# Agent attention with a cosine feed-forward on one core: two bursts of exponentials a batch instead of three

## The chip, the core and the metric

The kernel runs on one core of a Trainium2 chip. The metric is the device time of one execution in microseconds (us), the median of several runs. The engines are named as in the profile: PE (TensorE, matrix products), PEld (its weight loads), DVE (VectorE), ACT (ScalarE), POOL (GpSimd) and SP (SyncE, which issues transfers).

## What is computed

Cut from the reference, with B = 4 batches of N = 12480 tokens, C = 128 features, 49 agents and a hidden width of 2048:

```python
def sm(a, b):
    s = scale * (a @ b.transpose(0, 2, 1))
    s = s - s.max(-1, keepdims=True)
    e = np.exp(s)
    return e / (e.sum(-1, keepdims=True) + 1e-09)
agent_v = sm(agents, k) @ v
x = sm(q, agents) @ agent_v
...
h = x @ w_in
out = (h * np.cos(h)) @ w_out
```

So there are two softmaxes, one of the agents over all keys of a batch and one of each query over the 49 agents, and behind them a wide layer whose activation is h cos h.

## The kernel before

Queries and keys are taken in groups of 960 tokens (8 tiles of 120), 13 groups a batch and 52 in all. The product of a batch's agent values with w_in is made once a batch (`project`), into one of two tables `a`, so that the hidden layer of a group of queries is one product of that table with the group's transposed softmax weights `pT`.

**The main loop** goes over 832 steps. A group takes 16 steps, a batch 208. A step is a slice of 256 hidden units for 480 tokens: PE makes the first product into a buffer `ph` of PSUM (L853, two instructions, three buffers), ACT the cosine (L856, `c`), DVE the cubic part (L862, `r` = (cos - 1) h), and PE, four steps later, the second product (L878), which gathers 8 steps in one buffer `one`. There are two buffers `one`, and scores, values and transposes use the same two. The cubic part frees the step's `ph`.

**Around the steps lies the softmax work of what comes next**: the scores of keys and queries (`scores`, L152, one transfer and 8 products for a group), copied out of PSUM by ACT, or inside a burst by DVE (L527), the queries' maximum on DVE (L531) and its subtraction on POOL (L533), the running maximum of the keys (L250), and for the keys, once all 13 groups are scored, `top`, `across`, `spread`, `shift`: the maximum is spread over partitions (`mxb`, L271) and subtracted on POOL (L275). After the exponential the keys' groups go through `add` (POOL, L284 and L286, into `es`) and `values` (PE, L301, the products with v; DVE adds them up, L307 and L309). Queries go through their sums (L578) and reciprocals (L582, L583) on DVE, the weights on POOL (L591, `p`), a transpose on PE (L600), a copy on ACT (L604) and two casts and two differences on POOL (L607, L608) into `pT`.

**Bursts.** Exponential and sine lie in different tables of ACT, so a change between them costs a table load each way. The exponentials are therefore made in bursts: one exponential for a *piece* (some groups of queries, side by side in one tile `e`) and one for a *lot* (some groups of keys), between two table loads. The tuple `BURSTS` has the steps of a batch at which they stand; `pieces` says which groups of queries, `lots` which groups of keys. A burst is planned for step n; ACT reaches it after the cosine of step n + 1.

**The order** is written by hand. `plan(n, f)` runs f at step n, `early_plan` likewise ahead of the step's cubic part, `extra` puts it at the next free step of certain places among 8, and `spread_out` spreads a list over the steps up to an end. In a *window* of six steps from a burst on, PE, DVE and ACT keep the order in which the code was written (`as_traced`); `fill` puts there what DVE and PE are to do while ACT has the exponential's table: the piece's sums, and up to three items of the list `todo`, each a group of query scores ("q") or a group of values ("v").

Of the kernel before, what the change touches and what calls it, by code (L numbers as in the profile page):

```python
# [18 lines left out]
P = 128  # L19
TT = 120  # L20
# [22 lines left out]
def agent_attention_cos_ffn(ctx, tc, qT, kT, v, v0, v0_rest, agT, w_in, w_out, outT):  # L43
# [122 lines left out]
    class Weights:  # L166
# [43 lines left out]
        def turned(self, c):  # L210

            pt = self.psum()
            for t in range(4):
                f = slice((4 * c + t) * P, (4 * c + t + 1) * P)
                nc.tensor.transpose(pt[:, t * P:(t + 1) * P], win[:, f], ident)
            if c == 0:
                self.room = self.sb.tile([P, NF, P], F32, name="e", bufs=4)
            wt = self.done[c, 0] = self.room[:, 4 * c:4 * c + 4]
            nc.scalar.copy(wt.rearrange("p f d -> p (f d)"), pt)

# [255 lines left out]
    with ExitStack() as pools:  # L476
# [28 lines left out]
        NQ = NB * NG  # L505
        NSTEP = NB * PER
        e_of, rz_of = {}, {}
        PIECES = 5

        def query_parts(n, piece, wide=False, by_vector=False):  # L510
            b, g = n // NG, n % NG
            src = qT[b, :, g * GRP:(g + 1) * GRP]
            if wide:
                ps = scores_twice(sb.tile([P, 2 * 512], F32, name="xt", bufs=3)[:, :GRP], src, b, pair())
                yield
            else:
                ps = scores(sb, src, b, small()).rearrange("p (h t) a -> p h t a", h=2)
                yield
            if n == piece[0]:
                e = sb.tile([TT, PIECES * GT, NA], F32, name="e", bufs=4)  # L520
                rz = sb.tile([TT, PIECES * GT], F32, name="rz2", bufs=4)
                for i, k in enumerate(piece):
                    e_of[k], rz_of[k] = e[:, i * GT:(i + 1) * GT], rz[:, i * GT:(i + 1) * GT]
                    e_of[piece], rz_of[piece] = e[:, :len(piece) * GT], rz[:, :len(piece) * GT]
            e = e_of[n].rearrange("p (h t) a -> p h t a", h=2)
            if not wide:
                (nc.vector.tensor_copy if by_vector else nc.scalar.copy)(e, ps)  # L527
                ps = e
            mx = sb.tile([TT, GT], F32, name="mx2")
            mx = mx.rearrange("p (h t) -> p h t", h=2)  # L530
            nc.vector.reduce_max(mx, ps, axis=AX.X)  # L531
            on = nc.vector if wide else nc.gpsimd
            on.tensor_sub(e, ps, mx.unsqueeze(3).to_broadcast([TT, 2, HT, NA]))  # L533

        def query_first(n, piece):

            e = e_of[n] = sb.tile([TT, GT, NA], F32, name="e", bufs=4)
            rz = rz_of[n] = sb.tile([TT, GT], F32, name="rz2", bufs=4)
            ps = scores_twice(wide_tile()[:, :GRP], qT[0, :, n * GRP:(n + 1) * GRP], 0, pair())
            yield  # L540
# [78 lines left out]


        assert NG == 13
        BURSTS = (109, 133, 157)
        WINDOW = 6
        windows = set()

        def windows_late(n):
            return any(n - x in windows for x in (1, 2, 3, 4))

        first, early = (0, 1, 2), (3, 4, 5, 6, 7)
        pieces = [tuple(tuple(range(b * NG + x, min(b * NG + y, NQ))) for x, y in ((8, 12), (12, 16), (16, 21))  # L630
                        if b * NG + x < NQ) for b in range(NB)]
        lots = [(0, 4), (4, 4), (8, 5)]


        po_w = []
# [133 lines left out]
        for b in range(1, NB):  # L769
# [12 lines left out]
            t = extra(t, ab[b].across)  # L782
            t = extra(t + 1, ab[b].spread)
            assert t < o + BURSTS[0], (t, o)
            for g, n in lots:
                plan(t, ab[b].shift, g, n, nc.gpsimd)
            nxt = scored(pieces[b][0], False, True)[:2]
            ahead = len(nxt)
            fresh = [scored(ps[1], False, True), scored(ps[2], False, True), nxt]
            for k, at in enumerate(BURSTS):  # L790
                at += o
                burst(at, ps[k], (ab[b], *lots[k]))
                vs, qs = valued(k - 1) if k else [], fresh[k]
                todo = []
                for x in ("qqqqqqq", "vq", "vq")[k]:
                    z = vs if x == "v" else qs
                    if z:
                        todo.append(z.pop(0))
                fill(at, todo)
                t = at + 6  # L800
                if k == 2:
                    vs += valued(2)
                qs, todo = todo, []
                qs += [x for x in fresh[k] if x not in qs]
                qs = [x[:3] if x[0] is query else x for x in qs]
                while vs or qs:
                    todo += qs[:1] + vs[:1]
                    vs, qs = vs[1:], qs[1:]
                if k == 0:
                    todo += [x[:3] for x in fresh[1][:2]]  # L810
                    del fresh[1][:2]
                end = o + BURSTS[min(k + 1, 2)] - 4
                for i, x in enumerate(todo):
                    t = extra(t, *x, dense=k == 2) + (2 if k == 2 else 1)
                    assert k == 2 or x[0] is not query or t < o + BURSTS[k + 1], (t, o, k)
                    if k < 2 and i + 1 < len(todo):
                        t += max(0, (end - t) // (len(todo) - i - 1) - 1)
            plan(t, ab[b].total)
            t = extra(t, ab[b].folded) + 1
            t = extra(t, ab[b].inverse) + 1  # L820
# [240 lines left out]
```

## Time and profile before

| what | value |
|---|---|
| median of 3 runs | 1180.17 us (1177.71 to 1183.73) |
| profiled execution | 1180.92 us |
| its span, first to last instruction | 1179.1 us |
| busy: PE, DVE, ACT, POOL | 95%, 90%, 83%, 30% |
| cubic parts (L862) | 832, 916.1 us busy |
| cosines (L856) | 832, 785.3 us busy |
| loads of the exponential's table in bursts (L575) | 11 |

The span is made of the start, four batches of 208 steps and an end. A batch's extra work lies in the three first batches; the last has only its own remaining queries to prepare. Busy shares are averages over stretches with different limits. In rows of a timeline the first two numbers are the start and the duration in us, equal neighbours are merged (x2), and the bracket at the end is the engine's idle time before the row and what ended it.

### The profile page before, as it was taken

Reading aid. Unit: us, or ns where it says so; the run is one execution under the profiler, and the core shown is the slowest. Engines: PE = TensorE matmul, PEld = TensorE weight load, DVE = VectorE, ACT = ScalarE, POOL = GpSimd, SP = SyncE. Lnnn points to the kernel's source line nnn. Section 1 sums busy time; section 2 is a strip of 40 time slices with the busy share of each in tenths; the row PEclk is TensorE's granted clock in tenths of the full one; section 3 lists DMA queues with packets and bytes.
Section 4 is the critical chain, followed back from the end, with each engine's and each line's share of the span. In section 5 each row is a group of like instructions: output and inputs, shape, how many; then the busy total and the mean of one; then the engine's idle time right before and its main releaser. Section 6 shows DMA issues by size and latency. Waiting matters only on the chain.

```text
span 1179.1 us, 17151 instructions
## 1 busy us (share of the span) xinstructions
PE 1122.9 (95%) x6239; PEld 901.8 (76%) x6239; DVE 1061.0 (90%) x1205; ACT 980.1 (83%) x1234; POOL 349.9 (30%) x389
## 2 busy tenths in 40 slices
PE   6899999999999999999899999998999999989996
PEld 3677888787778888787777888877777777767774
DVE  5779999997899999998789999998878999999996
ACT  4778888898678888888778888898777899998995
POOL 1032131752313131463323122264331223122320
PEclk9999999998999999999899999999989999999998
DMA  9733324523201223263220322354240000000001
GB/s 362 288 93 108 101 84 135 167 85 106 96 34 54 91 74 95 81 181 114 85 84 17 101 67 84 106 152 130 68 118 34 34 34 18 34 17 34 18 34 37
DMA packets 37520, 107.74 MB, mean 91 GB/s; under 512 B 4162, under 2 KB 4770, under 8 KB 37426
## 3 DMA queue, kind: packets, MB, share of 16 engines
q1 hardware_dynamic: 37426, 106.55, 28.0%
q8 instruction: 52, 0.85, 0.3%
q14 instruction: 42, 0.34, 0.1%
HBM read 80.97 MB, written 25.56 MB: 90 GB/s over the span
## 4 chain that ended last, share of the span: by engine, by line
PE 70%; DVE 15%; ACT 9%; issue 4%; DMA 1%; SPq 0%; POOL 0%; ACTq 0%; DVEq 0%
PE ph L853 26%; PE one L878 22%; DVE r L862 12%; PE one L152 10%; ACT c L856 5%; PE one L301 3%; PE one L874 2%; PE one L600 2%; PE one L875 1%; DMA c<-qT 1%; PE ph L451 1%; PE one L346 1%; ACT osb L880 1%; ACT L575 1%; ACT s L279 1%
## 5 line engine op out<-in xcount | busy, mean ns | idle before, releaser
L862 DVE SCALAR_TENSOR_TENSOR r<-c,ph 128x960 fp32r<-128x960 f32 x832 | 916.1, 1148 | 60.3 <-ACT c L856 49.7
L856 ACT ACTIVATE c<-ph 128x960 f32<-128x960 f32 x832 | 785.3, 980 | 110.9 <-PE ph L853 99.3
L853 PE MATMUL ph<-pT,a 113*128 113x480 f32 x1664 | 540.2, 404 | 19.7 <-DVE r L862 18.4
L878 PE MATMUL one<-r,w 128*128 128x480 f32 x1664 | 505.4, 392 | 2.1 <-ACT osb L880 1.7
L853 PEld LDWEIGHTS ph<-pT,a 113*128 113x128 f32 x1664 | 293.8, 191 | 134.9 <-DVE r L862 73.6
L878 PEld LDWEIGHTS one<-r,w 128*128 128x128 f32 x1664 | 312.3, 192 | 54.9 <-issue 4.8
L152 PEld LDWEIGHTS one<-ag,xt 128*120 128x120 f32 x1408 | 164.3, 188 | 14.1 <-DVE sums L307 4.2
L152 PE MATMUL one<-ag,xt 128*120 128x49 f32 x1408 | 160.9, 268 | 5.5 <-DVE sums L307 3.0
L591 POOL TENSOR_TENSOR p<-e,rz 120x392 f32<-120x392 f32 x51 | 42.9, 846 | 323.7 <-PE one L600 252.2
L608 POOL TENSOR_TENSOR pT<-p,pT 49x480 fp32r<-49x480 f32 x102 | 124.2, 1217 | 7.8
L533 POOL TENSOR_TENSOR e<-e,mx 120x392 f32<-120x392 f32 x49 | 41.4, 844 | 225.9 <-DVE mx L531 225.6
L607 POOL CAST pT<-p 49x480 fp32r<-49x480 f32 x102 | 59.4, 583 | 114.7 <-ACT p L604 110.1
L880 ACT COPY osb<-one 128x480 f32<-128x480 f32 x104 | 57.9, 557 | 4.1 <-PE one L878 4.1
L301 PE MATMUL one<-vt,s 120*49 120x128 f32 (+1 forms) x624 | 44.9, 289 | 5.2 <-DVE sums L309 5.2
L301 PEld LDWEIGHTS one<-vt,s 120*49 120x49 f32 (+1 forms) x624 | 35.1, 136 | 17.9 <-issue 8.1
L286 POOL TENSOR_TENSOR es<-es,s 120x392 f32<-120x392 f32 x36 | 36.8, 1023 | 37.2 <-ACT s L279 35.5
L275 POOL TENSOR_TENSOR s<-s,mxb 120x1568 f32<-120x1568 f32 (+1 forms) x9 | 31.5, 3534 | 34.1 <-DVE mxb L271 34.1
L875 PE MATMUL one<-pT,b 113*128 113x480 f32 x104 | 39.9, 384 | 0.0
L874 PE MATMUL one<-pT,b 113*128 113x480 f32 x104 | 39.9, 384 | 0.0
L248 ACT COPY s<-one 120x392 f32<-120x392 f32 x36 | 17.5, 487 | 20.8 <-PE one L152 20.8
L527 ACT COPY e<-one 120x392 f32<-120x392 f32 x34 | 16.6, 487 | 20.3 <-PE one L152 20.3
L600 PEld LDWEIGHTS one<-ident,p 120*113 120x113 f32 x204 | 28.6, 179 | 4.6 <-ACT a L347 0.9
(143 smaller groups left out, 542.7 us busy)
## 6 DMA issues: line engine op xcount, KB each, us to landing
outT<-osb SPq DMA_DIRECT2D x51, 480.0 KB, 2.6
xt<-qT SPq DMA_DIRECT2D x49, 480.0 KB, 3.6
xt<-kT SPq DMA_DIRECT2D x39, 480.0 KB, 3.5
vt<-v SPq DMA_DIRECT2D x78, 240.0 KB, 3.9
xt<-kT SPq DMA_DIRECT2D x7, 512.0 KB, 7.7
vt<-v SPq DMA_DIRECT2D x6, 512.0 KB, 5.2
c<-kT SPq DMA_DIRECT2D x5, 512.0 KB, 6.9
vt<-w_in SPq DMA_DIRECT2D x8, 256.0 KB, 7.2
```

The costliest lines, as they stand in the source:

```text
L152: mm = nc.tensor.matmul(ps[:, t, :], xt[:, t * TT:(t + 1) * TT], ag[:, b, :], start=True, stop=True)
L301: mm = nc.tensor.matmul(po[h * HI:h * HI + width], e[:, x * NA:x * NA + width], vt[:, x, :], start=(t == 0), stop=(t == HT - 1))
L600: mm = nc.tensor.transpose(pt[:KR, t * TT:(t + 1) * TT], p_in[n % 2][:, t, :KR], ident[:TT, :TT])
L607: nc.gpsimd.tensor_copy(pT[own, c], p[own])
L608: nc.gpsimd.tensor_sub(pT[other, c], p[own], pT[own, c].bitcast(F32))
L853: nc.tensor.matmul(ph[:, j, :CH], ai[:, f], pTs[q % 3][:, c], start=True, stop=True)
L856: nc.scalar.activation(cos, h, AF.Sin, bias=HALF_PI, scale=1.0)
L862: nc.vector.scalar_tensor_tensor(r, cos, 1.0, h, op0=ALU.subtract, op1=ALU.mult)
L874: nc.tensor.matmul(po, b1[k], pTs[q % 3][:, c], start=False, stop=False)
L875: nc.tensor.matmul(po, b2[k], pTs[q % 3][:, c], start=False, stop=False)
L878: nc.tensor.matmul(po, w1[:, f, :], r[:, j, :], start=(f == 0), stop=(f == NF - 1))
L880: nc.scalar.copy(osb[:, c * CH:(c + 1) * CH], po)
```

## The change

Each batch has two bursts, at steps 97 and 142, instead of three at 109, 133 and 157. The pieces become 6 and 7 groups of queries (of 4, 4 and 5), the lots 7 and 6 groups of keys (of 4, 4 and 5). The tile `e` holds seven groups instead of five and has three buffers instead of four; the three first groups share one. The shift of the keys is cut into four parts (4, 3, 3, 3) instead of three. Three groups of the next batch's queries are scored ahead instead of two, and two groups of the first lot's values wait for the second window, whose list is "qvq". The exponentials cover the same elements.

```diff
-        PIECES = 5
+        PIECES = 7
...
-                e = sb.tile([TT, PIECES * GT, NA], F32, name="e", bufs=4)
+                e = sb.tile([TT, PIECES * GT, NA], F32, name="e", bufs=3)
...
-            e = e_of[n] = sb.tile([TT, GT, NA], F32, name="e", bufs=4)
+            if n == 0:
+                e_of["first"] = sb.tile([TT, 3 * GT, NA], F32, name="e", bufs=3)
+            e = e_of[n] = e_of["first"][:, n * GT:(n + 1) * GT]
...
-        BURSTS = (109, 133, 157)
+        BURSTS = (97, 142)
...
-        pieces = [tuple(tuple(range(b * NG + x, min(b * NG + y, NQ))) for x, y in ((8, 12), (12, 16), (16, 21))
+        pieces = [tuple(tuple(range(b * NG + x, min(b * NG + y, NQ))) for x, y in ((8, 14), (14, 21))
...
-        lots = [(0, 4), (4, 4), (8, 5)]
+        lots = [(0, 7), (7, NG - 7)]
...
-            for g, n in lots:
+            for g, n in ((0, 4), (4, 3), (7, 3), (10, 3)):
                 plan(t, ab[b].shift, g, n, nc.gpsimd)
-            nxt = scored(pieces[b][0], False, True)[:2]
+            nxt = scored(pieces[b][0], False, True)[:3]
             ahead = len(nxt)
-            fresh = [scored(ps[1], False, True), scored(ps[2], False, True), nxt]
+            fresh, kept = scored(ps[1], False, True), []
             for k, at in enumerate(BURSTS):
                 at += o
                 burst(at, ps[k], (ab[b], *lots[k]))
-                vs, qs = valued(k - 1) if k else [], fresh[k]
+                vs, qs = kept, fresh
                 todo = []
-                for x in ("qqqqqqq", "vq", "vq")[k]:
+                for x in ("qqq", "qvq")[k]:
...
-                if k == 2:
-                    vs += valued(2)
...
+                vs += valued(k)
+                if k == 0:
+                    vs, kept = vs[:-2], vs[-2:]
+                end = o + (BURSTS + (182,))[k + 1] - 4
...
-                    t = extra(t, *x, dense=k == 2) + (2 if k == 2 else 1)
+                    t = extra(t, *x, dense=k == 1) + 1
```

On ACT, at the first burst of the second batch, the order before is this; `e` is a piece and `s` a lot, and the numbers are partitions x elements.

```order
L856 ACTIVATE c<-ph 128x2x480 x2
L880 COPY osb<-one 128x480
L856 ACTIVATE c<-ph 128x2x480 x2
L575 ACT_TABLE_LOAD
L575 ACTIVATE e<-e 120x1568
L279 ACTIVATE s<-s 120x1568
L856 ACT_TABLE_LOAD
L856 ACTIVATE c<-ph 128x2x480 x5
```

At the first burst of the second batch of the change ACT has this order:

```order
L880 COPY osb<-one 128x480
L856 ACTIVATE c<-ph 128x2x480 x7
L577 ACT_TABLE_LOAD
L577 ACTIVATE e<-e 120x2352
L279 ACTIVATE s<-s 120x2744
L856 ACT_TABLE_LOAD
L856 ACTIVATE c<-ph 128x2x480 x2
```

Both exponentials are longer, and between the copy of a group's output and the burst seven cosines stand instead of two.

On DVE, at the third burst of the second batch, the order before is this; `rz` is the sums of a piece, `one` is scores for L527 and values for L309.

```order
L862 SCALAR_TENSOR_TENSOR r<-c,ph 128x960 x6
L309 TENSOR_TENSOR sums<-sums,one 113x128 x2
L578 TENSOR_REDUCE rz_5225<-e 120x8 x2
L527 COPY e<-one 120x392
L531 TENSOR_REDUCE mx_5726<-e 120x8
L578 TENSOR_REDUCE rz_5225<-e 120x8 x3
L862 SCALAR_TENSOR_TENSOR r<-c,ph 128x960 x5
```

At the second and last burst of the second batch of the change DVE has this order:

```order
L309 TENSOR_TENSOR sums<-sums,one 113x128
L862 SCALAR_TENSOR_TENSOR r<-c,ph 128x960
L527 COPY e<-one 120x392
L531 TENSOR_REDUCE mx_5546<-e 120x8
L580 TENSOR_REDUCE rz_4885<-e 120x8 x2
L309 TENSOR_TENSOR sums<-sums,one 113x128
L580 TENSOR_REDUCE rz_4885<-e 120x8 x5
L862 SCALAR_TENSOR_TENSOR r<-c,ph 128x960 x2
```

The copy of the scores stands ahead of the sums instead of among them, one addition of values has moved ahead of the last cubic part, and the sums are seven instead of five.

On POOL, from the shift of the second batch on, the order before is this; `e` in L533 is a group of queries, `es` the sum of the keys' exponentials, `p` the weights of a group and `pT` what PE reads.

```order
L275 TENSOR_TENSOR s<-s,mxb 120x1568 x2
L275 TENSOR_TENSOR s<-s,mxb 120x1960
L607 CAST pT_97<-p 49x480 x2
L608 TENSOR_TENSOR pT_97<-p,pT_97 49x480 x2
L533 TENSOR_TENSOR e<-e,mx_4993 120x392
L284 COPY es<-s 120x392
L286 TENSOR_TENSOR es<-es,s 120x392
L533 TENSOR_TENSOR e<-e,mx_5017 120x392
L286 TENSOR_TENSOR es<-es,s 120x392 x2
L533 TENSOR_TENSOR e<-e,mx_5052 120x392
```

From the shift of the second batch of the change on, POOL has this order:

```order
L275 TENSOR_TENSOR s<-s,mxb 120x1568
L275 TENSOR_TENSOR s<-s,mxb 120x1176 x3
L533 TENSOR_TENSOR e<-e,mx_4887 120x392
L533 TENSOR_TENSOR e<-e,mx_4911 120x392
L284 COPY es<-s 120x392
L286 TENSOR_TENSOR es<-es,s 120x392 x6
L533 TENSOR_TENSOR e<-e,mx_4952 120x392
L593 TENSOR_TENSOR p_102<-e,rz_2754 120x2x4x49
L593 TENSOR_TENSOR p_101<-e,rz_2754 120x2x4x49
L533 TENSOR_TENSOR e<-e,mx_5001 120x392
L609 CAST pT_97<-p 49x480 x2
L610 TENSOR_TENSOR pT_97<-p,pT_97 49x480 x2
```

The next `pT` stood right behind the shift and now stands behind all of the lot's additions, two products and four subtractions. In both versions it is the one that PE needs at step 112.

## Rows read from the trace of the kernel before

**Rows 1.** The page, part 1: busy us (share of the span) and instructions.

```profile
PE 1122.9 (95%) x6239; PEld 901.8 (76%) x6239; DVE 1061.0 (90%) x1205; ACT 980.1 (83%) x1234; POOL 349.9 (30%) x389
```

**Rows 2.** Stretches: length, busy PE PEld DVE ACT POOL, clock, DMA; second batch, two third bursts.

```profile
365.50:648.00 282.50, 275.07 (x1579) 227.91 (x1579) 259.04 (x288) 239.01 (x286) 93.83 (x99) 0.98 0.30 91
...
288.00:301.00 13.00, 11.43 (x50) 9.63 (x50) 7.08 (x13) 8.89 (x8) 5.89 (x6) 0.61 0.39 115
...
569.00:587.00 18.00, 14.65 (x83) 12.03 (x83) 12.53 (x19) 13.59 (x14) 7.10 (x7) 0.81 0.28 82
```

**Rows 3.** Timeline of DVE, first burst of the second batch.

```profile
497.88 2.22 DVE L862 SCALAR_TENSOR_TENSOR r<-c,ph 128x960 fp32r<-128x960 f32 x2 [0.17 <-ACT c L856]
...
500.68 0.56 DVE L531 TENSOR_REDUCE mx<-e 120x8 f32<-120x392 f32 x1
501.56 1.03 DVE L578 TENSOR_REDUCE rz<-e 120x8 f32<-120x392 f32 x2 [0.32 <-ACT e L575]
...
505.25 2.22 DVE L862 SCALAR_TENSOR_TENSOR r<-c,ph 128x960 fp32r<-128x960 f32 x2 [0.53 <-ACT c L856]
```

**Rows 4.** Timeline of DVE, second burst of the second batch.

```profile
533.21 2.22 DVE L862 SCALAR_TENSOR_TENSOR r<-c,ph 128x960 fp32r<-128x960 f32 x2 [0.17 <-ACT c L856]
...
540.58 1.15 DVE L862 SCALAR_TENSOR_TENSOR r<-c,ph 128x960 fp32r<-128x960 f32 x1 [0.58 <-ACT c L856]
```

**Rows 5.** Timeline of DVE, third burst of the second batch.

```profile
567.10 4.41 DVE L862 SCALAR_TENSOR_TENSOR r<-c,ph 128x960 fp32r<-128x960 f32 x4 [0.59 <-ACT c L856]
...
579.69 5.48 DVE L862 SCALAR_TENSOR_TENSOR r<-c,ph 128x960 fp32r<-128x960 f32 x5
585.09 0.18 DVE L582 TENSOR_SCALAR rz<-rz 120x40 f32<-120x40 f32 x1
586.42 1.15 DVE L862 SCALAR_TENSOR_TENSOR r<-c,ph 128x960 fp32r<-128x960 f32 x1 [1.15 <-ACT c L856]
```

**Rows 6.** Timeline of DVE, third burst of the first batch.

```profile
287.82 1.15 DVE L862 SCALAR_TENSOR_TENSOR r<-c,ph 128x960 fp32r<-128x960 f32 x1
288.89 0.28 DVE L309 TENSOR_TENSOR sums<-sums,one 113x128 f32<-113x128 f32 x1
...
296.21 0.57 DVE L527 COPY e<-one 120x392 f32<-120x392 f32 x1 [3.74 <-PE one L152]
...
298.76 2.21 DVE L862 SCALAR_TENSOR_TENSOR r<-c,ph 128x960 fp32r<-128x960 f32 x2
```

**Rows 7.** Timeline of DVE, third burst of the third batch.

```profile
862.85 0.57 DVE L527 COPY e<-one 120x392 f32<-120x392 f32 x1 [3.74 <-PE one L152]
```

**Rows 8.** Timeline of ACT, first burst of the second batch.

```profile
498.73 1.28 ACT L575 ACT_TABLE_LOAD   x1
...
504.25 2.79 ACT L856 ACTIVATE c<-ph 128x960 f32<-128x960 f32 x3
```

**Rows 9.** Groups by line and shape: busy us, mean ns | idle before.

```profile
L575 ACT ACT_TABLE_LOAD x11 | 14.1, 1283 | 0.2
...
L575 ACT ACTIVATE e<-e 120x1568 f32<-120x1568 f32 x7 | 10.6, 1511 | 0.1
...
L575 ACT ACTIVATE e<-e 120x1960 f32<-120x1960 f32 x4 | 7.3, 1836 | 0.0
...
L583 DVE RECIPROCAL rz<-rz 120x32 f32<-120x32 f32 x7 | 2.4, 341 | 0.0
```

**Rows 10.** Timeline of PE, third burst of the second batch.

```profile
575.31 1.79 PE L152 MATMUL one<-ag,xt 128*120 128x49 f32 x16
```

**Rows 11.** Timeline of POOL, shift and first burst of the second batch.

```profile
491.44 10.51 POOL L275 TENSOR_TENSOR s<-s,mxb 120x1568 f32<-120x1568 f32 x3 [13.48 <-DVE mxb L271]
...
503.19 2.49 POOL L608 TENSOR_TENSOR pT<-p,pT 49x480 fp32r<-49x480 f32 x2
...
507.14 1.03 POOL L286 TENSOR_TENSOR es<-es,s 120x392 f32<-120x392 f32 x1
...
513.37 1.65 POOL L591 TENSOR_TENSOR p<-e,rz 120x392 f32<-120x392 f32 x2 [1.50 <-DVE rz L583]
```

More of the change, by code (lines that the diff above doesn't have):

```diff
@@ L216, in turned @@
             if c == 0:
-                self.room = self.sb.tile([P, NF, P], F32, name="e", bufs=4)
+                self.room = self.sb.tile([P, NF, P], F32, name="e", bufs=3)
             wt = self.done[c, 0] = self.room[:, 4 * c:4 * c + 4]
@@ L800, in agent_attention_cos_ffn @@
                 t = at + 6
-                if k == 2:
-                    vs += valued(2)
-                qs, todo = todo, []
-                qs += [x for x in fresh[k] if x not in qs]
-                qs = [x[:3] if x[0] is query else x for x in qs]
+                qs = [x[:3] for x in qs]
+                vs += valued(k)
+                if k == 0:
+                    vs, kept = vs[:-2], vs[-2:]
+                end = o + (BURSTS + (182,))[k + 1] - 4
+                todo = []
                 while vs or qs:
@@ L808, in agent_attention_cos_ffn @@
                     vs, qs = vs[1:], qs[1:]
[L809 to L812, printed above, removed]
                 for i, x in enumerate(todo):
-                    t = extra(t, *x, dense=k == 2) + (2 if k == 2 else 1)
-                    assert k == 2 or x[0] is not query or t < o + BURSTS[k + 1], (t, o, k)
-                    if k < 2 and i + 1 < len(todo):
+                    t = extra(t, *x, dense=k == 1) + 1
+                    if i + 1 < len(todo):
                         t += max(0, (end - t) // (len(todo) - i - 1) - 1)
+                assert k or t <= at - o + o + BURSTS[1] - BURSTS[0], (t, o)
+                fresh = nxt
             plan(t, ab[b].total)
```

## Prediction

> **What bounds the kernel now.** I read the busy shares first. PE is busy 95% and DVE 90% of the span [rows 1], so neither has much to give, and ACT, on which the exponentials run, isn't the fullest. The table by stretch says the same of one batch: in the second, of 282.5 us, PE has work in 275.07 and DVE in 259.04 [rows 2]. DVE runs one cubic part (L862) a step and everything else between them; a batch can't be shorter than DVE's work plus the time in which DVE is kept from it. So the question is where DVE goes without cubic parts, and the timeline of DVE around each burst of exponentials answers it.
>
> While ACT loads the exponential's table, runs two exponentials and loads the sine's table again, no cosine is made. DVE finishes the cubic parts whose cosines are there and then has only what the program put into the burst: sums of the exponentials, and copies and maxima of the scores that PE makes meanwhile. I call the time from the end of the last cubic part before to the start of the next one a gap. In the second batch the first burst's gap runs from 497.88 + 2.22 = 500.10 to 505.25, 5.15 us [rows 3], the second's from 535.43 to 540.58, 5.15 us [rows 4]. The third is longer: 571.51 to 579.69, 8.18 us, and six steps later DVE waits once more, 1.15 us, for a late cosine [rows 5]. In the first batch the third gap is 288.97 to 298.76, 9.79 us [rows 6], with a wait of 3.74 us of DVE's copy for PE's scores; the third batch has the same 3.74 [rows 7], and I take 9.79 there too. The first two bursts I take at 5.15 in all three batches.
>
> The third gap isn't long for ACT's sake. PE makes two groups of values there before the scores that DVE's copy waits for, and the granted clock is low: 0.61 of full speed in that stretch of the first batch, in which PE is busy for 11.43 of 13.00 us, and 0.81 in the second's [rows 2]. A part of it therefore ran at the lower of the two levels, 1.2 GHz instead of 2.4.
>
> **The change, part by part.** *What goes.* Three batches lose one burst of three each. Six gaps of 5.15, two of 9.79 and one of 8.18 + 1.15 make 59.8 us in which cubic parts stood still.
>
> *What comes in their place.* Six bursts, each longer. Between the two starts that bracket it, 498.73 (table load) and 504.25 (first cosine after), the old first burst keeps ACT for 5.52 us [rows 8]. It held 1568 + 1568 elements; the new ones hold 2352 + 2744 or 2744 + 2352, so 1960 more. 392 more elements cost 1836 - 1511 = 325 ns [rows 9], or 0.83 ns each, so 1.63 us, and the block becomes 7.15 us. DVE's last cubic part ended 1.37 us after the block began (500.10 against 498.73), and the next began 1.00 us after it ended (505.25 against 504.25) [rows 3, 8]. With both kept, a gap is 7.15 + 1.00 - 1.37 = 6.78 us, and six are 40.7 us. Saved: 59.8 - 40.7 = 19.1 us.
>
> This holds if DVE's own list fits into the gap. The new first burst has two pairs of copy and maximum (0.57 + 0.56 each [rows 3, 6]) and six sums (1.03 for two), 5.3 us; the second has one pair, seven sums and one addition of 0.28, 5.0 us. The sums can't start before the query exponential is done: 1.28 + 2.16 us after the block's start in the first, 1.28 + 2.49 in the second (1511 ns and 0.83 ns for each element more [rows 9]). Counted from there, the first list ends at 3.44 + 1.03 + 1.13 + 2.06 = 7.7 us and the second at 3.77 + 3.6 + 0.3 = 7.7, and the first new cosine is ready at 8.15. So ACT ends both gaps, with half a microsecond to spare.
>
> *The same work elsewhere.* Of each batch's copies and maxima four pairs lay in gaps and three do now; of the additions of values (0.28 each) three did and one does. So 1.13 + 0.56 = 1.7 us a batch, 5.1 us in all, moves to where cubic parts run. Its bounds are 0, where PE sets the pace and DVE has room, and the full 5.1. I take the full sum, since DVE is at 259 of 282.5 in a batch.
>
> *Fewer small operations.* Each piece of queries needs an addition and a reciprocal after its sums, 0.18 + 0.34 us [rows 5, 9]. There were twelve pieces and now are eight: 2.1 us saved.
>
> *The clock.* A longer burst starves PE longer. The same list took 9.79 us at clock 0.61 and 8.18 at 0.81 [rows 2, 5, 6], so a deeper fall costs about 1.6 us. I let it fall on two of the six bursts, 3.2 us; the bounds are none and all six, 9.6 us.
>
> *Moved earlier.* Scores of keys and queries must now be spread up to step 83 of a batch instead of 95. In the second batch 13 groups stand from step 6 to 86 where 15 stood from 2 to 96, the same density, so nothing. In the first, two more groups of queries stand ahead of the burst and two fewer behind it; the PE time that is free behind it pays for them, and if it doesn't they cost 2 x 1.79 = 3.6 us once [rows 10]. One group of query scores goes from the last batch to the first, at most 1.79 us either way. I take all of it at nothing.
>
> The sum: -19.1 + 5.1 - 2.1 + 3.2 = -12.9 us. The profiled execution took 1180.92 us, 0.75 above the median of the runs, so **1168.0 us**.
>
> *A rule beside the rows.* The trace shows a table load of 1283 ns [rows 9] and the exponential starting right behind it, so a burst fewer saves ACT 2.6 us of loads. The Trainium skill ("ScalarE: Activation LUTs", What ACT_TABLE_LOAD costs) puts a switch of tables at about 2.66 us, with a drain of 1.38 us behind the load. By that estimate three bursts fewer would save ACT another 8.3 us; the rows show no such drain, and the sum stands by them.
>
> **The rivals.** *Nothing measurable.* The new second burst might end as the third did, by PE: it too begins with a group of values, scores, and values again. Then its gap is 9.79 instead of 6.78, 3.0 us more a batch, and with the clock falling in each first burst (1.6) it is 4.6 us a batch, 13.8 in all, on 1164.8 us (the sum without the clock's term): **1178.6 us**. For it speaks that PE gets little to do in a block of 7.15 us, and that its clock fell to 0.61 in such a stretch [rows 2]. Against it: in the third burst both groups of values stood ahead of the scores that DVE's copy waits for, and now one group stands ahead and one behind them. It decides if the copy comes more than about 2 us late: it can be made 1.65 us after the block's start (1.37 for the last cubic part, 0.28 for an addition of values), the sums behind it begin at 3.77 in any case, and half a microsecond is spare. The Trainium skill ("TensorE: Matmul & The Clock Gate", Part 1) has a rule that speaks for this rival: the array's clock is throttled by default and released by activity. By it a longer stretch with little work for PE is the wrong direction. The 0.61 of the third burst agrees with it.
>
> *Much faster.* PE is the fullest engine, and in the three third bursts its clock took 13 x 0.39 = 5.1 us twice and 18 x 0.19 = 3.4 us once [rows 2] of PE's time. If PE sets the pace between the bursts, the moved 5.1 us cost nothing, no new fall comes, and a third of those 13.6 us, 4.5, is won besides: 1180.9 - 19.1 - 2.1 - 4.5 = **1155 us**. Against it: DVE's idle in the gaps is what goes, and little else.
>
> *Slower.* POOL takes one queue in order. Before, the transposed weights of the next queries (CAST and TENSOR_TENSOR into pT) stood ahead of the additions of the key exponentials; now two subtractions, a copy and six additions in a row stand ahead of the pT that PE needs at step 112. The shift (L275) takes 10.51 us and began 7.29 us before the table load [rows 8, 11]; now four steps lie between instead of six, 1.1 us each (5.48 for five cubic parts [rows 5]), so it ends 5.7 us after the block's start, and the key exponential at 5.9. From there: two subtractions at about 0.83 (as long as the products of the same shape, 1.65 for two), 0.5 and six additions of 1.03, a subtraction, two products, a subtraction, two casts (from 501.95 to 503.19) and one of the two differences (2.49 for both) [rows 11]. The products wait for the reciprocal, which comes behind six cubic parts and a pair, 8.15 + 6 x 1.1 + 1.13 + 0.5 = 16.4. So pT is there 21.5 us after the block's start. PE wants it when the cubic part of step 109 frees its buffer: 8.15 + 11 x 1.1 + 2.2 for copies and maxima, 22.4. So there is 0.9 us of room; beyond it each microsecond costs one in each batch. To be slower by 0.5%, 12.9 + 5.9 us must go, 6.3 a batch, so pT has to be 7.2 us later than this; at 8 it is **1189 us**. No row lets me expect that chain to be a third longer.
>
> **How the numbers follow.** About 0.5%, 5.9 us, is what a measurement can tell from no change, so faster means below 1174.3 and slower above 1186.1. The forecast has 0.55; its own range, from the bounds of the moved work and the clock, is 1160 (both 0) to 1174 (5.1 and 9.6). Much faster has 0.15, nothing measurable 0.2, slower 0.1. The first two make faster 0.67; the third and the forecast's edge make 0.24 for the same; slower is 0.09. For 8 in 10 the range leaves out the far half of the fast case and the slow one: 1156 to 1181.
>
> **What would show it.** Each of the six gaps of DVE should be 6.5 to 7.1 us, with ACT's cosine, not PE's scores, ending it; ACT's block should be 7.1 to 7.2. Eight loads of each table from L577 and the line of cosines. The clock should be 1.0 through most first bursts. The wrong steps would show as: a copy (L527) in the second burst that waits for PE; a first product that waits for POOL's pT at step 112; ACT's key exponential waiting for the shift. The prediction fails if the steps outside the bursts get slower by more than 1.7 us a batch, since all of the gain is in the bursts.

## The result, and the profile after

The changed kernel takes **1164.68 us** (median of 4 runs, 1163.32 to 1166.43) against 1178.94 in the runs of the kernel before beside it. The ratio is 0.9871, with a 95% interval of 0.9844 to 0.9897: faster, by more than the half per cent that a measurement can tell. The profiled execution took 1164.66 us with a span of 1162.9, against 1180.92 and 1179.1, so 16.3 us less.

From the page of the changed kernel, part 1 (as [rows 1]):

```profile
PE 1111.1 (96%) x6239; PEld 886.9 (76%) x6239; DVE 1061.3 (91%) x1197; ACT 972.4 (84%) x1221; POOL 350.8 (30%) x392
```

DVE has as much work as before. PE has as many products, but is busy for 11.8 us less: more of the products ran at the higher clock. The table by stretch shows it too, for the second batch and then for its two bursts (columns as in [rows 2]):

```profile
364.90:642.10 277.20, 271.45 (x1578) 224.13 (x1578) 259.35 (x285) 236.18 (x282) 94.30 (x100) 1.00 0.30 93
484.70:493.00 8.30, 7.61 (x53) 6.21 (x51) 6.52 (x13) 8.24 (x7) 8.30 (x5) 1.00 0.80 224
549.50:557.80 8.30, 8.09 (x62) 6.61 (x62) 6.00 (x13) 8.24 (x7) 3.04 (x4) 1.00 0.64 176
```

The batch is 5.3 us shorter than that of [rows 2], the clock is 1.00 instead of 0.98, and inside both bursts PE has work nearly all the time. The timeline of DVE in these two bursts (as [rows 3] and [rows 4]):

```profile
482.88 3.28 DVE L862 SCALAR_TENSOR_TENSOR r<-c,ph 128x960 fp32r<-128x960 f32 x3
486.07 0.56 DVE L527 COPY e<-one 120x392 f32<-120x392 f32 x1
...
492.91 2.22 DVE L862 SCALAR_TENSOR_TENSOR r<-c,ph 128x960 fp32r<-128x960 f32 x2 [0.63 <-ACT c L856]
...
549.54 1.15 DVE L862 SCALAR_TENSOR_TENSOR r<-c,ph 128x960 fp32r<-128x960 f32 x1
551.52 0.57 DVE L527 COPY e<-one 120x392 f32<-120x392 f32 x1 [0.83 <-PE one L152]
...
557.68 2.22 DVE L862 SCALAR_TENSOR_TENSOR r<-c,ph 128x960 fp32r<-128x960 f32 x2 [0.77 <-ACT c L856]
```

The first gap is 492.91 - 486.16 = 6.75 us, the second 557.68 - 550.69 = 6.99. Both end with a wait for ACT's cosine. The copy in the second waits 0.83 us for PE's scores, and the cosine still comes last. The timeline of ACT in the first burst (as [rows 8]):

```profile
484.75 1.28 ACT L577 ACT_TABLE_LOAD   x1
486.04 2.17 ACT L577 ACTIVATE e<-e 120x2352 f32<-120x2352 f32 x1
488.11 2.48 ACT L279 ACTIVATE s<-s 120x2744 f32<-120x2744 f32 x1
490.61 1.28 ACT L856 ACT_TABLE_LOAD   x1
491.90 1.83 ACT L856 ACTIVATE c<-ph 128x960 f32<-128x960 f32 x2
```

The block is 491.90 - 484.75 = 7.15 us. Last, the queue of POOL and the PE that waits for it, first burst of the second batch (as [rows 11]); the row of PE is the first product with the new `pT`:

```profile
505.81 2.50 POOL L610 TENSOR_TENSOR pT<-p,pT 49x480 fp32r<-49x480 f32 x2
```

```profile
507.99 0.60 PE L853 MATMUL ph<-pT,a 113*128 113x480 f32 x2
```

The first of the two subtractions ends at about 505.81 + 1.25 = 507.06, so 0.9 us ahead of its reader, which has no wait.

### The profile page after: what moved, and what is told of

The parts are those of the page before. It is cut to its first block, busy times and chain, and to the rows that moved or that the text cites. A ratio compares the mean times of both kernels' runs of the same rounds, so it can differ in the third digit from the quotient of the medians.

```text
span 1162.9 us, 17144 instructions
## 1 busy us (share of the span) xinstructions
PE 1111.1 (96%) x6239; PEld 886.9 (76%) x6239; DVE 1061.3 (91%) x1197; ACT 972.4 (84%) x1221; POOL 350.8 (30%) x392
## 4 chain that ended last, share of the span: by engine, by line
PE 71%; DVE 13%; ACT 10%; issue 3%; DMA 2%; SPq 0%; POOL 0%; ACTq 0%; DVEq 0%
PE ph L853 27%; PE one L878 23%; DVE r L862 11%; PE one L152 10%; ACT c L856 5%; PE one L301 3%; PE one L874 2%; PE one L875 2%; PE one L602 1%; DMA c<-qT 1%; ACT e L577 1%; PE ph L451 1%; PE one L346 1%; ACT s L279 1%; ACT L577 1%
## 5 line engine op out<-in xcount | busy, mean ns | idle before, releaser
L853 PE MATMUL ph<-pT,a 113*128 113x480 f32 x1664 | 534.2, 402 | 15.5 <-DVE r L862 13.4
L878 PE MATMUL one<-r,w 128*128 128x480 f32 x1664 | 497.8, 388 | 5.3 <-ACT osb L880 3.6
L853 PEld LDWEIGHTS ph<-pT,a 113*128 113x128 f32 x1664 | 288.6, 189 | 133.3 <-DVE r L862 79.2
L878 PEld LDWEIGHTS one<-r,w 128*128 128x128 f32 x1664 | 308.1, 189 | 57.4 <-ACT p L606 5.0
L152 PEld LDWEIGHTS one<-ag,xt 128*120 128x120 f32 x1408 | 160.4, 185 | 16.2 <-DVE sums L309 5.5
L152 PE MATMUL one<-ag,xt 128*120 128x49 f32 x1408 | 158.0, 265 | 6.2 <-DVE sums L309 3.3
L533 POOL TENSOR_TENSOR e<-e,mx 120x392 f32<-120x392 f32 x49 | 41.2, 845 | 197.1 <-DVE mx L531 197.1
L527 ACT COPY e<-one 120x392 f32<-120x392 f32 x34 | 16.6, 488 | 20.6 <-PE one L152 20.6
L275 POOL TENSOR_TENSOR s<-s,mxb 120x1176 f32<-120x1176 f32 (+1 forms) x12 | 31.8, 2693 | 4.1 <-DVE mxb L271 4.1
```

What stands on the lines that cost most here:

```text
L152: mm = nc.tensor.matmul(ps[:, t, :], xt[:, t * TT:(t + 1) * TT], ag[:, b, :], start=True, stop=True)
L853: nc.tensor.matmul(ph[:, j, :CH], ai[:, f], pTs[q % 3][:, c], start=True, stop=True)
L878: nc.tensor.matmul(po, w1[:, f, :], r[:, j, :], start=(f == 0), stop=(f == NF - 1))
```

## The experiments

The scheme of a burst's list, which the code gives to `fill`, matters in all of them: q is a group of query scores, v a group of values (for PE 1.79 and 1.09 us). Before, the three lists were qqqqqqq (of which three are placed in the burst), vq and vq; the change has qqq and qvq. The batches' lengths, from the first cubic part of one batch to that of the next in the timeline of DVE of each profiled execution, tell where time goes. A profiled execution can lie some us off its median, three_fed's by 5.2.

| kernel | batch 1 | batch 2 | batch 3 | median us |
|---|---|---|---|---|
| before | 298.98 | 282.53 | 284.13 | 1178.94 |
| after | 298.72 | 277.19 | 275.18 | 1164.68 |
| three_mended | 298.69 | 283.63 | 280.93 | 1177.54 |
| three_fed | 300.15 | 279.68 | 279.19 | 1168.33 |
| values_first | 298.73 | 277.19 | 275.19 | 1164.88 |
| short_lists | 301.99 | 281.13 | 282.61 | 1179.23 |
| short_idle | 300.73 | 279.27 | 278.49 | 1172.22 |
| bare_burst | 305.68 | 280.13 | 278.05 | 1177.41 |
| pool_late | 305.68 | 279.61 | 282.18 | 1179.57 |
| last_idle | 298.69 | 277.31 | 275.16 | 1163.61 |
| second_full | 302.08 | 277.99 | 277.57 | 1166.91 |
| first_full | 298.79 | 276.31 | 274.21 | 1161.83 |
| both_full | 299.58 | 279.15 | 277.81 | 1168.40 |

**Three bursts, the third one's gap mended.** If gaps of DVE make the time, the three long third gaps can be had without merging bursts. In the kernel before, the list of the third burst is turned round, and the places of a burst are reserved beforehand so that no group of values stands right ahead of it:

```diff
+                taken.update(range(o + at, o + at + 3))
...
-                for x in ("qqqqqqq", "vq", "vq")[k]:
+                for x in ("qqqqqqq", "vq", "qv")[k]:
```

> The kernel before with its three bursts, where the third burst's window takes scores ahead of values and no group of values stands right ahead of the window's first step. Theory of the gaps (the gain came from the time in which DVE's cubic parts stand still): the third gap is then ended by ACT, at its block of 6.16 us, 6.16 + 1.00 - 1.37 = 5.8 us instead of 9.79, 9.34 and 9.79, so 11.5 us come off, to a ratio of 0.990 against the kernel before, most of what the change gave, with as many bursts as ever. Rival, the number of bursts (each costs its two table loads, 2.57 us of ACT, and a stop): nothing changes, 1.000.

Measured: 1177.54 us, ratio 0.9976 (0.9958 to 0.9994). The third gaps did become 5.81 us in all three batches, 10.3 us less in all, and only some 2.8 us came of it. The timeline of PE behind the third burst of the second batch says why:

```profile
577.04 0.60 PE L880 MATMUL one<-r,w 128*128 128x480 f32 x2
580.74 1.14 PE L855 MATMUL ph<-pT,a 113*128 113x480 f32 x2 [3.09 <-DVE r L864]
581.80 1.97 PE L301 MATMUL one<-vt,s 120*64 120x128 f32 x16
583.70 1.17 PE L880 MATMUL one<-r,w 128*128 128x480 f32 x2
```

and the table of that burst and of what follows it, by stretch:

```profile
572.25:580.00 7.75, 4.92 (x35) 3.62 (x34) 5.61 (x11) 7.71 (x6) 3.63 (x5) 0.99 0.27 63
580.00:587.00 7.00, 6.26 (x27) 4.85 (x28) 4.36 (x6) 3.07 (x4) 2.44 (x3) 0.52 0.30 80
```

PE runs out of its list, waits 3.09 us, and then, with everything to catch up on, works at a granted clock of 0.52, nearly all of it the lower level, 1.2 GHz. The group of values that takes 1.09 us takes 1.97. So the accounting by gaps alone falls (it gave 0.990), and so does its rival, no change at all; most of what the gap gave, PE lost behind it. This made a new theory: a burst costs what PE can't do in it, and the clock that it loses by that.

**Three bursts, with enough for PE.** The same kernel, with one more group of scores in the second and the third list:

```diff
-                for x in ("qqqqqqq", "vq", "qv")[k]:
+                for x in ("qqqqqqq", "qvq", "qvq")[k]:
```

> The three bursts of before, as in three_mended, but the second and the third burst get one more group of query scores for PE (lists qvq, qvq instead of vq, qv). Theory A (a burst in which PE runs out of work costs time behind it, by the work that it still has to do and by its clock): PE's idle stretch of 3.1 us in the third burst of three_mended falls under 1.5 us, no stretch at the lower clock follows it, and 3 to 4 us a batch come back in the eight steps after it: 1166 to 1170 us, ratio to before 0.988 to 0.993. Theory B (the number of bursts and their gaps set the time): gaps are 5.15, 5.15 and 5.8 as in three_mended, so 1177 us, ratio 0.9975.

Measured: 1168.33 us, ratio 0.9898 (0.9874 to 0.9921). Theory A gave 1166 to 1170. The gaps of DVE are those of three_mended but for one, 5.15 to 5.16 and 5.81 us (the profiled execution, the slowest of the five, has a fall of the clock in its very first burst). PE's wait in the third burst, timeline of PE:

```profile
577.87 0.60 PE L880 MATMUL one<-r,w 128*128 128x480 f32 x2
579.15 0.70 PE L855 MATMUL ph<-pT,a 113*128 113x480 f32 x2 [0.68 <-DVE r L864]
```

0.68 us instead of 3.09. The stretch behind it has 33 products where three_mended had 27, at 0.76 instead of 0.52:

```profile
580.00:587.00 7.00, 6.31 (x33) 5.36 (x34) 5.55 (x9) 3.62 (x5) 1.89 (x3) 0.76 0.25 73
```

So with three bursts a batch the kernel has most of what the change brought, if with more in its lists: seven groups of scores and two of values a batch, where the change has five and one. How much of the step from 1177.54 us is the clock and how much the work that now lies in the bursts, this run doesn't tell; short_idle, below, takes the two apart for the changed kernel. The expectation was too hopeful in one thing: a fall still follows that burst, only a shorter one.

**Two bursts, with too little for PE.** The other way round: the changed kernel with one group of scores fewer in each burst. The group comes later, among the steps.

```diff
-                for x in ("qqq", "qvq")[k]:
+                for x in ("qq", "qv")[k]:
```

> The changed kernel with one group of query scores fewer in each of the six bursts (lists qq and qv instead of qqq and qvq; the group comes later, among the steps). Theory A: the gaps stay at 6.75 and 6.99, since ACT ends them, but PE idles some 3 us in each of them instead of 1.1, low clock follows some of them, and each costs 2 to 3.5 us in the steps behind it: 1177 to 1186 us. Theory B: same gaps, same work: 1164 to 1167 us.

Measured: 1179.23 us, ratio 0.9990 (0.9973 to 1.0007). All of the gain is gone, with two bursts and with gaps of 6.75 and 7.0 us (one of six is 7.7, and six steps behind another burst the cubic parts stand still for 3.7 us once more). First burst of the third batch, timeline of PE, and the stretch behind the burst:

```profile
779.08 1.17 PE L853 MATMUL ph<-pT,a 113*128 113x480 f32 x2 [2.87 <-DVE r L862]
780.04 1.00 PE L878 MATMUL one<-r,w 128*128 128x480 f32 x2
...
783.24 3.28 PE L152 MATMUL one<-ag,xt 128*120 128x49 f32 x16
```

```profile
777.90:789.00 11.10, 9.92 (x33) 8.82 (x34) 7.82 (x9) 6.23 (x8) 8.73 (x10) 0.54 0.25 78
```

The same group of scores that takes PE 1.79 us elsewhere takes 3.28 here.

**Is it the clock, or the work that is pushed out?** The same kernel with eight products whose result nobody reads in the place of the missing group:

```diff
+        def idle_scores(b):
+            ps = small()[:TT, :GT * NA].rearrange("p (t a) -> p t a", a=NA)
+            for t in range(GT):
+                mm = nc.tensor.matmul(ps[:, t, :], ident[:, :TT], ag[:, b, :], start=True, stop=True)
...
-                fill(at, todo)
+                fill(at, todo + [(idle_scores, b)])
```

> As short_lists, with eight products whose result nobody reads (1.8 us of PE) in place of the group taken out of each burst. If PE's clock is what the empty lists cost, it stays at 1.0 and the time returns to within 4 us of the changed kernel: 1165 to 1169. If it is the score work that is pushed out of the bursts (6 x 1.79 = 10.7 us of PE among the steps), it costs what short_lists costs: 1175 or more. A mixture lies between, in the share of each.

Measured: 1172.22 us, ratio 0.9937 (0.9917 to 0.9957): a mixture, in nearly equal parts. 7.0 of the 14.55 us that short_lists lost come back by products that do nothing but keep PE busy, and 7.5 stay, 1.25 for each of the six groups that were pushed out. That is rather an upper bound: in the batches 1 and 2, where the clock is 1.00, the table shows 2.0 and 2.1 us for two groups, and in the third, where it falls in the second burst, 3.3. First burst of the third batch again, PE's first row behind it and the stretch from there:

```profile
775.20 0.70 PE L860 MATMUL ph<-pT,a 113*128 113x480 f32 x2 [0.64 <-DVE r L869]
```

```profile
774.00:785.00 11.00, 10.36 (x57) 8.70 (x56) 11.00 (x12) 9.80 (x13) 10.53 (x13) 1.00 0.27 90
```

57 products instead of 33 in eleven microseconds, at the upper level.

**The order within the second list.** 

> The changed kernel with one edit: the second window's list is values, scores, scores instead of scores, values, scores, so that two groups of values stand ahead of the scores that DVE copies first. Theory of the gaps: the second gap, 6.99 us in the changed kernel, is then ended by PE as the old third one was, at 8.2 to 9.8 us, which is 3.6 to 8.4 us in three batches, a ratio of 0.990 to 0.994 against the kernel before (the changed kernel has 0.987); the clock may fall there. Rival, a block of 7.14 us is long enough to hide any order: 0.987.

```diff
-                for x in ("qqq", "qvq")[k]:
+                for x in ("qqq", "vqq")[k]:
```

Measured: 1164.88 us, ratio 0.9867 (0.9838 to 0.9895), and a gap of 7.07 instead of 6.99. The timeline of PE, second burst of the second batch, shows both groups of values ahead of the scores (the first ends at 547.76, ahead of these rows), as they stood in the third burst of before:

```profile
549.49 1.09 PE L301 MATMUL one<-vt,s 120*64 120x128 f32 x16 [1.09 <-DVE sums L309]
...
551.49 1.78 PE L152 MATMUL one<-ag,xt 128*120 128x49 f32 x16
```

The loss that was forecast for this order, 3.6 to 8.4 us, did not come. In this list it doesn't matter whether the scores or the values come first.

**A change of tables by itself.** One more table load each way, with an exponential of a single element between them, at step 120 of each of the three first batches:

```diff
+        def bare():
+            t = sb.tile([1, 1], F32, name="bare", bufs=1)
+            tc.keep_in_program_order(nc.scalar.activation(t, ones[:1], AF.Exp))
...
+            plan(o + 120, bare)
```

> The changed kernel with a third switch of tables a batch, at step 120: one exponential of a single element between the two loads, and no list of work for the window. Theory of the gaps: ACT's block is 2 x 1.28 + 0.2 = 2.8 us, DVE's gap 2.8 + 1.00 - 1.37 = 2.4 us without work of its own, so 7.2 us in three batches, a ratio of 0.993. Rival, ACT at 84% has room for two loads: below 2 us in all, 0.988. Rival, each burst costs a fixed 5 us or more whatever it holds (restart of the chain from PE to DVE): 15 us, 1.000.

Measured: 1177.41 us, ratio 0.9969 (0.9951 to 0.9986): 12.7 us more than the changed kernel, which lies between the forecasts of 7.2 and 15. The timeline of ACT shows the block, 247.84 - 245.03 = 2.81 us; that of DVE a wait of 2.64:

```profile
245.03 1.28 ACT L617 ACT_TABLE_LOAD   x1
246.32 0.20 ACT L617 ACTIVATE bare<-ones 1x1 f32<-1x1 f32 x1
246.55 1.28 ACT L861 ACT_TABLE_LOAD   x1
247.84 0.97 ACT L861 ACTIVATE c<-ph 128x960 f32<-128x960 f32 x1
```

In the second and the third batch that costs 2.9 us a batch, in the first 7.0. The table by stretch holds what differs, the first batch above the second:

```profile
245.00:261.00 16.00, 14.16 (x52) 11.79 (x51) 9.29 (x10) 11.03 (x15) 5.26 (x6) 0.68 0.11 32
529.30:545.30 16.00, 13.95 (x83) 11.10 (x82) 12.83 (x14) 14.36 (x19) 5.27 (x6) 1.00 0.19 59
```

So one stop of the same length (PE waits 1.81 to 1.83 us in all three batches) costs about the length of ACT's block where the clock stays, and 4.1 us more where the clock is 0.68 of full speed over these 16 us. In the 16 us ahead of the stop PE was busy without a break at a clock of 1.00 in all three. Why it fell behind one of them is not shown.

**POOL made late.** Four additions of zeros, 4.1 us, stand ahead of the `pT` of step 112, which has 0.9 us to spare:

```diff
+            if g in (2, 3, 4, 5):
+                nc.gpsimd.tensor_add(self.es, self.es, nought)
```

> The changed kernel with four additions of zeros (about 1.03 us each on POOL, 4.1 us a batch) among the key additions that stand ahead of the pT of step 112. In the changed kernel's trace that pT was 0.9 us early. Theory of the prediction's slower rival: 4.1 - 0.9 = 3.2 us of stall for PE's first product in each of three batches, 9.6 us, a ratio of 0.995. Rival, the pipeline behind PE (three buffers ph, four steps to the second product) swallows such a stall: under 2 us in all, 0.988.

Measured: 1179.57 us, ratio 0.9993 (0.9975 to 1.0011): 14.9 us more than the changed kernel, beyond both forecasts (9.6, or under 2). PE stops where it was expected, for 2.07 us instead of 3.2 (timeline of PE, first batch):

```profile
233.01 0.71 PE L858 MATMUL ph<-pT,a 113*128 113x480 f32 x2 [2.07 <-POOL pT L615]
```

The second batch loses 2.4 us by it, the first and the third 7.0. The table by stretch, 16 us around the stop, in the first and the second batch:

```profile
230.00:246.00 16.00, 13.93 (x62) 11.62 (x61) 8.77 (x10) 7.85 (x10) 4.88 (x6) 0.68 0.26 89
514.50:530.50 16.00, 13.94 (x85) 11.73 (x84) 12.94 (x15) 11.34 (x15) 5.48 (x7) 1.00 0.36 118
```

The third batch has 0.68 too, from 794 to 810 us. The same picture: 2.4 for the stop, 4.6 for the clock.

**Keeping PE busy in the last burst**, where in the changed kernel it waits 3.72 us and 3.4 us at half clock follow: two lots of the useless products. The wait, timeline of PE:

```profile
1031.95 0.71 PE L853 MATMUL ph<-pT,a 113*128 113x480 f32 x2 [3.72 <-DVE r L862]
```

```diff
-        fill(at, [])
+        fill(at, [(idle_scores, NB - 1)] * 2)
```

> The changed kernel with two lots of eight products whose result nobody reads (3.6 us of PE) in the last burst, in which PE idles 3.72 us and after which 3.4 us run at half clock. If the fall of the clock costs what it takes, about half of 3.4 us plus what queues behind it, 1 to 2.5 us come off: 1162 to 1164. If the steps behind that burst are set by ACT and DVE, nothing: 1164.7.

Measured: 1163.61 us, ratio 0.9867 (0.9844 to 0.9890). The stretch behind that burst, first of the changed kernel, then of this one:

```profile
1030.10:1037.10 7.00, 5.14 (x16) 4.02 (x17) 6.76 (x9) 5.59 (x8) 0.00 (x0) 0.76 0.17 70
```

```profile
1030.00:1037.00 7.00, 6.05 (x28) 4.42 (x27) 7.00 (x9) 6.60 (x9) 0.00 (x0) 1.00 0.17 70
```

The clock there is 1.00 instead of 0.76, and the last batch, which has no other difference, is 232.08 us long from its first cubic part to its last instead of 233.52: the fall was worth 1.4 us. The median agrees, but its interval doesn't exclude nothing.

**Longer lists still.** In all three the products of last_idle stay, and `fill` places up to four entries.

> last_idle (1163.6) with a fourth entry in the second burst (lists qqq and qvqv): a group of values, 1.09 us of PE and an addition of 0.28 of DVE, goes into the 1.0 us in which PE idles at the end of that burst. If PE's work sets the pace outside the bursts, up to 1.0 us a batch comes off: 1160.5 to 1162.5. If the addition delays the cubic parts behind the burst (DVE has 1.7 us to spare in that gap), or DVE sets the pace: 1163 to 1165.

> last_idle (1163.6) with a fourth group of query scores in the first burst (lists qqqq and qvq): 1.79 us of PE against the 1.2 us in which it idles there, and 1.1 us of copy and maximum for DVE, which has 1.7 us to spare in that gap. If PE's pace decides: 1.2 us a batch, 1160 to 1162. If the copy comes behind the first cosine (the list then ends about 8.8 us after the table load, the cosine comes at 8.2), each burst loses 0.6 us or so and PE gives it back: 1163 to 1166.

> last_idle (1163.6) with both: qqqq and qvqv. If PE's pace decides, the two gains add up: 1157 to 1161. If DVE is late by them: 1163 to 1167.

The edit of first_full; second_full has "qvqv" in the second list instead, and both_full has both:

```diff
-            parts = [in_parts(*todo.pop(0)) for _ in range(min(3, len(todo)))]
+            parts = [in_parts(*todo.pop(0)) for _ in range(min(4, len(todo)))]
...
-                for x in ("qqq", "qvq")[k]:
+                for x in ("qqqq", "qvq")[k]:
```

Measured: second_full 1166.91 us, ratio 0.9878 (0.9857 to 0.9900); first_full 1161.83, 0.9832 (0.9809 to 0.9855); both_full 1168.40, 0.9901 (0.9875 to 0.9927). A fourth group of scores in the first burst brings 1.0 us in each of the batches 2 and 3, near the 1.2 us that PE idles there, and nothing in batch 1, whose second gap is 7.88 us long; it is the fastest version that ran, but its interval overlaps with that of the changed kernel. The fourth entry in the second burst, the group of values, does harm, and not in either of the ways expected. Timeline of PE, third batch of second_full:

```profile
838.23 0.60 PE L860 MATMUL ph<-pT,a 113*128 113x480 f32 x2
841.81 1.51 PE L301 MATMUL one<-vt,s 120*64 120x128 f32 x14 [2.99 <-DVE e L527]
```

The values wait for a buffer whose scores DVE copies only behind two cubic parts, PE's queue stands for 2.99 us, and behind it the clock is 0.76 from 839 to 846 us. Batch 1 loses 3.4 us and batch 3 2.4; batch 2, in which the clock stays at 1.00 there, loses 0.7. With both entries the losses outweigh the gains. An entry only helps if it can start.

## Why the prediction was right, and what in it was not

1168.0 us was forecast, with a range from 1156 to 1181; it is 1164.7. Step by step:

**The gaps** came out as worked out: a block of 7.15 for 7.15, and six gaps of 6.75 or 6.99 for 6.78, 41.2 us for 40.7. ACT ends them, as the text said.

**The moved work**, taken at its full 5.1 us from bounds of 0 and 5.1, has its size from short_idle: a group pushed out of a burst costs 1.0 to 1.25 us of time. One group a batch makes 3.0 to 3.8, and the six additions, which were not measured by themselves, would make 1.7 at full price, 5.4 in all at most. The choice of the upper bound was nearer than the lower one.

**Fewer small operations** were over-estimated: a merged reciprocal is longer, 498 ns for 56 elements where one of 32 took 341 [rows 9]. From the groups of the changed kernel by line and shape:

```profile
L585 DVE RECIPROCAL rz<-rz 120x56 f32<-120x56 f32 x3 | 1.5, 498 | 0.0
L585 DVE RECIPROCAL rz<-rz 120x48 f32<-120x48 f32 x3 | 1.3, 440 | 0.0
L585 DVE RECIPROCAL rz<-rz 120x40 f32<-120x40 f32 x2 | 0.8, 393 | 0.0
```

That is 3.6 us; seven of 341, four of 392 and one of 197 ns were 4.2. The additions (L582, now L584) took 5.1 us and take 4.4: 0.18 us is the shortest of them and not the usual one. So 1.3 us were saved instead of 2.1.

**The clock** is the term that had the wrong size. "A longer burst starves PE longer" is the step that failed: a burst starves PE by what its list lacks. With three entries PE's longest wait in the window of the second batch's first burst is the one of this row, behind the gap:

```profile
494.24 0.48 PE L878 MATMUL one<-r,w 128*128 128x480 f32 x1 [1.18 <-ACT osb L880]
```

The 3.2 us of surcharge did not occur: one fall lies in a second burst, that of the third batch (granted clock 0.66 from 828 to 833 us), and its gap is 6.99 like the others. Nor was the clock a cost at all. Half of what short_lists lost came back by keeping PE busy, and the runs of one and the same kernel say the like: of 56 runs of the kernel before, the 18 with the lowest granted clock (0.974 to 0.977) take 1182.6 us on average and the 17 with the highest (0.982 to 0.986) 1177.5. The four runs of the changed kernel have 0.990 to 0.993. A line through the 56 falls by 0.69 us for each 0.001 of clock; carried on to 0.9915 it gives 1172.2 us, so about 8 us of the gain go along with the clock. That is an estimate from beyond the range of the 56, and it doesn't tell how far the clock is the cause and how far it is the sign of a PE that waits.

**The sum.** With gaps -18.6, moved work 3.0 to 5.4, small operations -1.3 and no surcharge, it is -14.5 to -16.9 us; the medians differ by 14.3, the profiled executions by 16.3. That it fits is in part luck. It counts the gaps in full, which three_mended refutes, and the clock at nothing, which short_idle refutes; the two overlap, since the third gaps of before were themselves longer for the fall of the clock.

**"So nothing" for the moved scores** does not hold for each batch. Scores went from the third and the last batch to the first, shown by the table by stretch for L152 alone (16 products are a group; batches 1 to 3, before and then after):

```profile
66.49:365.47 298.98, 61.79 (x536) 0.98 0.32 96
365.47:648.00 282.53, 46.54 (x418) 0.98 0.30 91
648.00:932.13 284.13, 48.00 (x418) 0.98 0.29 91
```

```profile
67.18:365.91 298.73, 66.48 (x592) 1.00 0.34 103
365.91:643.10 277.19, 46.72 (x416) 1.00 0.30 93
643.10:918.28 275.18, 43.05 (x384) 0.99 0.28 87
```

So batch 1, which takes on 56 products, gains 0.3 us, and batch 3, which gives up 34, gains 8.9. Batch 2 has the same work and gains 5.3; the last batch, with 16 products instead of 42, gains 2.9. What the move is worth over all four is not shown.

**The rivals.** "Slower" named the right place and the margin, 0.9 us (its own terms add up to 1.1), and pool_late confirmed that lateness there costs time. Its price, one microsecond for each, holds at most while the clock stays: there the 3.2 us of lateness that were worked out stopped PE for 2.06 and cost 2.4, and where the clock fell the same cost 7.0. "Nothing measurable" did not come to pass, but the reason given against it, that one group of values stands ahead of the scores and one behind, isn't what decided: values_first has both ahead of them, with a gap of 7.07 us and the same time. "Much faster" was right that PE wins some of its clock back, and wrong that the moved work costs nothing.

**What the prediction did not see** is what its gaps depend on. It took the kernel for one in which DVE's gaps add up, and the fewer the bursts the better. The experiments show that a gap saved is time saved only if PE has work throughout it: three_mended shortens gaps by 10.3 us and gains 2.8; three_fed leaves them and gains 9 more; short_lists keeps the short total of the changed kernel and loses everything. By the medians three bursts with fuller lists come within 1168.33 - 1164.68 = 3.7 us of the change, and the intervals of the two ratios, 0.9874 to 0.9921 and 0.9844 to 0.9897, overlap. That is not the price of a third burst, since three_fed holds more work in its bursts than the change; two and three bursts with equal lists were not compared. The rest probably lies in the lists and in what PE waits for, but that is argued and not shown: in the third burst of before PE was held ahead of its second group of values, as this row of PE's timeline shows (second batch), and ran that group mostly at the lower clock. Of the new bursts the second begins with a wait of that kind too, of 1.09 to 1.11 us, and has enough behind it.

```profile
571.76 1.86 PE L301 MATMUL one<-vt,s 120*64 120x128 f32 x16 [1.72 <-DVE sums L309]
```

How much of the change each of its lines brought can't be told closer than that.

## What to carry to other kernels

When an engine's stop is shortened, look at what the other full engine does meanwhile: time comes back only if its queue has enough that can start. Count the entries of each burst in microseconds of the fullest engine, and make sure that none of them waits for a buffer that is freed only behind the burst. A gain that a merge seems to bring may belong to the lists that were rewritten along with it, so change the lists alone first. And read the granted clock of each run beside its time: a forecast can come out by terms that are wrong in opposite ways.

## What the runs showed of the hardware

A stop of PE of 1.8 to 2.1 us had two prices in different batches of one and the same program: 2.9 or 7.0 us in bare_burst, 2.4 or 7.0 in pool_late. The dearer ones are those behind which the granted clock was 0.68 over 16 us; a fall costs 4.1 to 4.6 us there. The shorter fall of the last burst, 0.76 over 7 us, was worth 1.4. The Trainium skill ("TensorE: Matmul & The Clock Gate", Part 1) says that the array's clock is throttled by default and released by activity; short_idle agrees: with products without a use the clock behind a burst was 1.00 where it had been 0.54, and 7.0 us came back.

ACT's change of table showed no cost beside its load: in bare_burst the exponential starts 1.29 us after a load of 1.28 begins, and both loads with the exponential take 2.81 us. The 1.38 us of drain that the Trainium skill ("ScalarE: Activation LUTs", What ACT_TABLE_LOAD costs) counts beside a load is in no row here.
